# Attention for one query, forward and backward: another order of DRAM blocks over the SBUF partitions

## The chip, the core and the metric

The kernel runs on one NeuronCore of a Trainium2 chip. Its time is the device time of one execution in microseconds (us). Three runs of the kernel before took 642.05, 642.48 and 642.67 us, so the median is 642.48 us.

The engines are TensorE (PE, matmul; its weight loads are listed as PEld), VectorE (DVE), ScalarE (ACT), GpSimd (POOL) and SyncE (SP). In this kernel SP does nothing but issue DMAs. Sixteen DMA engines carry them out.

## The reference

For each of 32 heads there is one query row, 8192 key rows and 8192 value rows of 128 numbers in bf16. The output is the attention, and from the gradient of the output the gradients of q, k and v are computed:

```
scores = q . k^T * 128**-0.5        # 1 x 8192 for each head
p      = softmax(scores)
out_0  = p . v                      # 1 x 128
dp     = grad_out . v^T             # 1 x 8192
ds     = p * (dp - sum(p * dp)) * 128**-0.5
out_1  = dq = ds . k                # 1 x 128
out_2  = dk = ds^T x q              # 8192 x 128 for each head
out_3  = dv = p^T x grad_out        # 8192 x 128 for each head
```

K and V are read once and dK and dV are written once. Each of these four is 2 MB for a head and 67 MB in all. So 134 MB are read and 134 MB are written. The other arrays are 8 KB each.

All sums over keys run over all 8192 of them, and everything else is done for each key by itself. The order in which the keys lie on chip therefore does not matter, as long as K, V, dK and dV share it.

## The kernel before

One head's K is a tile `Kt` of 128 partitions with `NT` = 64 rows of 128 bf16 each, which is 16 KB in a partition. `Vt` (V), `G_dk` and `G_dv` (the gradients) have the same shape. `rows_of` (line 69) is the DRAM side of every transfer of these four: partition p holds the 64 rows from 64p on, a contiguous block of 16 KB, and the block of partition p + 1 follows it directly.

`load_k` and `load_v` (lines 77 and 83) issue the loads, one transfer of 2 MB for each head and tensor. Only the first K is loaded in four parts of 512 KB, each with 4 KB in a partition. `outer` (line 249) computes a gradient tile in four quarters on VectorE and stores it with one transfer of 2 MB; for the first and the last head it uses two of 1 MB, with 8 KB in a partition.

The loop over `h` runs through 33 steps. In step h the scores, the softmax, the products with V and dV of head h are computed; and for head h - 1 the rest: ds, dq and dK. The order of instructions on each engine is the order in which the code is written (`tc.manual_schedule`). SP's order of DMAs follows from it: in the steady part it is a load of K, a store of dK, a load of V, a store of dV.

There are three buffers for K and two each for V, `G_dk` and `G_dv`. A load waits until the last reader of its buffer is done (for K the matmuls of dq at line 231, for V the transposes at line 197 or the matmuls of the output). A store waits for VectorE's last quarter (line 256), and VectorE waits for a store to land before it writes that buffer again.

On chip the rows are worked on by `k_blocks` (line 162, 32x32 transposes on VectorE), `k_scores` (line 177), `v_transposes` (line 197), `v_scores` (line 207) and `contract` (line 231). They address partitions and slots of the tiles and never a place in DRAM.

Of the kernel before, what the change touches and what calls it, by code (L numbers as in the profile page):

```python
# [15 lines left out]
CH = 16  # L16
# [9 lines left out]
def kernel(  # L26
# [12 lines left out]
    P = 128  # L39
# [28 lines left out]

    def rows_of(x, h, c, parts):
        L = NT // parts  # L70
        return x[0, h].rearrange("(p n) d -> p n d", p=P)[:, c * L:(c + 1) * L, :]

    def slots(X, c, parts):
        L = NT // parts
# [2 lines left out]
    def load_k(h):  # L77
        Kt[h] = kpool.tile([P, NT, D], BF16, tag="K", name="Kt")
        parts = NCH if h == 0 else 1
        for c in range(parts):  # L80
            nc.sync.dma_start(slots(Kt[h], c, parts), rows_of(k, h, c, parts))

    def load_v(h):
        Vt[h] = vpool.tile([P, NT, D], BF16, tag="V", name="Vt")
        nc.sync.dma_start(Vt[h][:], rows_of(v, h, 0, 1))
# [163 lines left out]
    def outer(h, which, r):  # L249
        x = st[h]  # L250
        if r == 0:
            x[which] = gpool.tile([P, NT, D], BF16, tag=which, name="G_" + which)
        G, dst = x[which], out_2 if which == "dk" else out_3
        rep, row = x["ds"] if which == "dk" else x["p"], qd[h][:, 0 if which == "dk" else 1, :]
        Q = NT // 4
        nc.vector.tensor_tensor(  # L256
            slots(G, r, 4).rearrange("p n (a b) -> p n a b", b=R),
            slots(rep, r, 4).unsqueeze(2).to_broadcast([P, Q, D // R, R]),
            row.rearrange("p (a b) -> p a b", b=R).unsqueeze(1).to_broadcast([P, Q, D // R, R]),
            op=ALU.mult)  # L260
        parts = 1
        if h == 0 or h == H - 1:
            parts = 2
        if r % (4 // parts) == 4 // parts - 1:
            c = r // (4 // parts)
            nc.sync.dma_start(rows_of(dst, h, c, parts), slots(G, c, parts))
# [37 lines left out]
    for h in range(H + 1):  # L304
        p_ = h - 1
        if h < H:
            x = st[h] = {}
# [121 lines left out]
```

## Time and profile before

| | |
|---|---|
| median of three runs | 642.48 us |
| the profiled execution | 642.33 us |
| its span, first to last instruction | 640.5 us |
| VectorE busy | 546.7 us (85%) |
| TensorE busy | 466.5 us (73%) |
| ScalarE busy | 205.5 us (32%) |
| HBM read, written | 134.23 MB, 134.23 MB |
| packets of 16 KB in SP's queue | 15744 |

A profile has rows for the busy time of engines, for 40 equal slices of the span (each digit is the busy share in tenths), for the DMA queues with their packets and the share of the 16 DMA engines' time that these took, for the chain of work that ended last, and for groups of instructions by line. A transfer is split into packets, here one for each contiguous run, and the packets are shared out over the 16 DMA engines. The trace also holds one record for each packet with its start, its duration and its size, but not the engine that carried it.

### The profile page before, as it was taken

How to read it: one execution, taken by the hardware profiler on the slowest of the kernel's cores; microseconds unless marked ns; L12 is line 12 of the kernel's file. 1: busy time of each engine (PE TensorE's matmuls, PEld its weight loads, DVE VectorE, ACT ScalarE, POOL GpSimd, SP SyncE). 2: the span in 40 equal slices, each digit the busy share in tenths (PEclk: the TensorE clock that was granted, in tenths of full speed). 3: DMA queues.
4: the chain of work that ended last, by engine and by line, in shares of the span. 5: the costliest groups of instructions: out<-in, count | busy, mean ns of one | idle time of the engine just before them, and what ended most of it. 6: DMA issues, size and time to landing. Idle time of an engine off the chain costs nothing.

```text
span 640.5 us, 8426 instructions
## 1 busy us (share of the span) xinstructions
PE 466.5 (73%) x3336; PEld 276.5 (43%) x3336; DVE 546.7 (85%) x780; ACT 205.5 (32%) x507; POOL 7.1 (1%) x13
## 2 busy tenths in 40 slices
PE   3776778778877867887866867767877687676771
PEld 1444444445544533455533444434554344444351
DVE  6799999998999999988889888898888988889871
ACT  1433332234433322334421333313442133322240
POOL 4000000000000000000000000000000000000000
PEclk9979888887787899877899887898787888879875
DMA  8999999999999999999999999999999999999994
GB/s 353 421 415 427 429 431 426 425 433 426 429 431 427 429 431 427 430 429 429 431 427 432 428 425 437 427 424 436 428 425 435 428 426 434 426 430 433 427 405 193
DMA packets 19671, 269.01 MB, mean 420 GB/s; under 512 B 2352, under 2 KB 2352, under 8 KB 2864
## 3 DMA queue, kind: packets, MB, share of 16 engines
q1 hardware_dynamic: 19536, 268.46, 98.6%
q8 instruction: 26, 0.43, 0.3%
q14 instruction: 13, 0.11, 0.0%
q10 hardware_dynamic: 96, 0.02, 0.0%
HBM read 134.23 MB, written 134.23 MB: 419 GB/s over the span
## 4 chain that ended last, share of the span: by engine, by line
DMA 45%; DVE 39%; PE 9%; ACT 4%; issue 1%; DVEq 0%; ACTq 0%
DMA Kt<-in_k_dram 45%; DVE XK_sb L162 15%; DVE G_dv L256 9%; DVE G_dk L256 7%; PE s_ps L177 3%; DVE dpT L214 2%; PE T_ps L197 2%; PE acc_ds L231 2%; ACT XV_sb L188 2%; DVE sT L184 1%; ACT p_rep L371 1%; DVE prod L217 1%; DVE ds L285 1%; ACT qd L273 1%; DVE four L125 1%
## 5 line engine op out<-in xcount | busy, mean ns | idle before, releaser
L197 PE MATMUL T_ps<-ident_f,Vt 128*128 128x128 f32 x1024 | 178.0, 339 | 1.0 <-DMA Vt<-in_v_dram 0.4
L256 DVE TENSOR_TENSOR G_dv<-p_rep,qd 128x2048 bf16<-128x2048 bf16 x128 | 148.2, 1220 | 35.3 <-DMA out_dram<-G_dv 28.1
L177 PE MATMUL s_ps<-XK_sb,win_q 128*128 128x512 bf16 x512 | 135.8, 397 | 50.1 <-DVE XK_sb L162 26.3
L197 PEld LDWEIGHTS T_ps<-ident_f,Vt 128*128 128x128 f32 x1024 | 151.4, 177 | 28.5 <-issue 20.1
L256 DVE TENSOR_TENSOR G_dk<-ds_rep,qd 128x2048 bf16<-128x2048 bf16 x128 | 154.7, 1210 | 1.1
L188 ACT COPY XV_sb<-T_ps 128x512 f32<-128x512 f32 x256 | 138.4, 586 | 53.2 <-PE T_ps L197 52.6
L162 DVE STREAM_TRANSPOSE XK_sb<-Kt 128x1024 f32<-128x1024 f32 x128 | 151.4, 1221 | 3.1 <-DMA Kt<-in_k_dram 2.9
L177 PEld LDWEIGHTS <-win_q 128*128 128x128 bf16 x512 | 52.7, 105 | 123.8 <-issue 83.2
L290 ACT COPY win_ds<-ds 128x64 bf16<-128x64 bf16 x32 | 7.8, 244 | 193.0 <-DVE ds L285 193.0
L355 ACT ACTIVATE e<-sT,nbias 128x64 f32<-128x64 f32 x32 | 13.0, 406 | 138.4 <-DVE nbias L350 138.4
L343 PE MATMUL m_ps<-ident_f,top 128*128 128x128 f32 x32 | 11.0, 342 | 60.3 <-DVE top L341 57.3
L207 PE MATMUL dp_ps<-XV_sb,do_win 128*32 128x512 bf16 x512 | 34.0, 382 | 24.7 <-ACT XV_sb L188 24.7
L231 PE MATMUL acc_p<-Vt,win_p 128*32 128x512 bf16 x512 | 48.3, 516 | 0.5 <-ACT win_p L372 0.5
L343 PEld LDWEIGHTS m_ps<-ident_f,top 128*128 128x128 f32 x32 | 4.5, 139 | 74.4 <-DVE top L341 72.9
L231 PE MATMUL acc_ds<-Kt,win_ds 128*32 128x512 bf16 x512 | 33.5, 382 | 0.9 <-ACT win_ds L290 0.9
L207 PEld LDWEIGHTS <-do_win 128*32 128x32 bf16 x512 | 14.2, 94 | 36.0 <-issue 29.5
L369 DVE RECIPROCAL rinv<-m_ps 128x1 f32<-128x1 f32 x32 | 5.4, 168 | 24.9 <-ACT qd L273 24.9
L184 DVE STREAM_TRANSPOSE sT<-s_ps 128x512 f32<-128x512 f32 x32 | 22.7, 709 | 3.6 <-PE s_ps L177 3.6
L356 PE MATMUL m_ps<-rs,ones_f 128*128 128x1 f32 x64 | 15.4, 310 | 11.5 <-ACT e L355 11.5
L231 PEld LDWEIGHTS <-win_p 128*32 128x32 bf16 x512 | 13.1, 117 | 23.8 <-issue 12.2
L214 DVE STREAM_TRANSPOSE dpT<-dp_ps 128x512 f32<-128x512 f32 x32 | 21.6, 675 | 0.8 <-PE dp_ps L207 0.8
L356 PEld LDWEIGHTS m_ps<-rs,ones_f 128*128 128x128 f32 x64 | 14.0, 272 | 17.8 <-ACT e L355 17.3
(57 smaller groups left out, 203.3 us busy)
## 6 DMA issues: line engine op xcount, KB each, us to landing
Vt<-in_v_dram SPq DMA_DIRECT2D x32, 2048.0 KB, 29.5
Kt<-in_k_dram SPq DMA_DIRECT2D x31, 2048.0 KB, 31.6
out_dram<-G_dv SPq DMA_DIRECT2D x30, 2048.0 KB, 34.8
out_dram<-G_dk SPq DMA_DIRECT2D x30, 2048.0 KB, 32.2
out_dram<-G_dv SPq DMA_DIRECT2D x4, 1024.0 KB, 11.6
out_dram<-G_dk SPq DMA_DIRECT2D x4, 1024.0 KB, 11.7
Kt<-in_k_dram SPq DMA_DIRECT2D x4, 512.0 KB, 5.6
out_dram<-fin_sb SPq DMA_DIRECT2D x2, 8.0 KB, 12.1
```

Of the source, the lines that this page charges most:

```text
L162: nc.vector.transpose(XK[h][:, :, :, u, :], slots(Kt[h], u, NCH).rearrange("p g d -> p (g d)").bitcast(F32).rearrange("p (g w j) -> p g w ...
L177: nc.tensor.matmul(st[h]["s"][:], lhsT=q_win[h % 2][:, c, at:at + P], rhs=cols[:, c // 2, u, c % 2], start=(u == 0 and c == 0), stop=(u == ...
L184: nc.vector.transpose(sT[:].rearrange("p g r -> p (g r)"), x["s"][:])
L188: nc.scalar.copy(XV[h][:, c * TB:(c + 1) * TB, :], st[h].pop(("T", c))[:])
L197: nc.tensor.transpose(T_ps[:, i, :], words[:, m * P:(m + 1) * P], ident_f[:])
L207: nc.tensor.matmul(out[b * QD:(b + 1) * QD, :], lhsT=do_win[:, h, e2, 2 - 2 * z:2 - 2 * z + QD], rhs=cols[:, z, e2, :, b * QD:(b + 1) * QD ...
L214: nc.vector.transpose(x["dpT"][:].rearrange("p m r -> p (m r)"), x["dp"][:])
L231: nc.tensor.matmul(acc[which][b * QD:(b + 1) * QD, :], lhsT=window(h, which)[:, g, at:at + QD], rhs=X[:, 4 * g:4 * g + 4, :].rearrange("p ...
L256: nc.vector.tensor_tensor(slots(G, r, 4).rearrange("p n (a b) -> p n a b", b=R), slots(rep, r, 4).unsqueeze(2).to_broadcast([P, Q, D // R, ...
L343: nc.tensor.transpose(x["m"][:, 128:256], top[:].to_broadcast([P, P]), ident_f[:])
L355: nc.scalar.activation(e[:].rearrange("p (u g) -> p u g", u=NCH), x["sn"], ACT.Exp, bias=nbias[:], scale=scale, accum_out=rs[:])
L356: nc.tensor.matmul(x["m"][:, 0:1], lhsT=ones_f[:], rhs=rs[:], start=True, stop=True, skip_group_check=True)
```

## The change

One line of `rows_of` is changed. A head's 128 blocks of 16 KB are numbered 16b + a, with a from 0 to 15 and b from 0 to 7, and block 16b + a now lies in partition 8a + b. Before, block p lay in partition p. So partitions 8a to 8a + 7 hold eight blocks that lie 256 KB apart in DRAM, and the partitions b, 8 + b, 16 + b and so on hold sixteen neighbouring blocks. Loads and stores use the same function, so K, V, dK and dV are moved alike and the outputs stand where they stood in DRAM.

```diff
     def rows_of(x, h, c, parts):
         L = NT // parts
-        return x[0, h].rearrange("(p n) d -> p n d", p=P)[:, c * L:(c + 1) * L, :]
+        return x[0, h].rearrange("(b a n) d -> a b n d", a=CH, b=P // CH)[:, :, c * L:(c + 1) * L, :]
```

`CH` is 16 and `P` is 128. The DRAM side of a transfer was one count of 128 with a contiguous run in it; it is two nested counts, 16 and 8, with the same run. The SBUF side is still 128 partitions. The words of the change are: "Partition 8a+b holds rows of DRAM block 16b+a: each DMA engine's 16 KB blocks lie 256 KB apart, neighbouring engines 16 KB apart".

## The prediction

> **What bounds the kernel now.** I read the busy shares of the engines first, then the DMA share slice by slice, then the queue's row, then the chain that ended last, and last the single packets.
>
> The head of the page, and its DMA rows:
>
> ```profile
> span 640.5 us, 8426 instructions
> PE 466.5 (73%) x3336; PEld 276.5 (43%) x3336; DVE 546.7 (85%) x780; ACT 205.5 (32%) x507; POOL 7.1 (1%) x13
> ...
> DMA  8999999999999999999999999999999999999994
> GB/s 353 421 415 427 429 431 426 425 433 426 429 431 427 429 431 427 430 429 429 431 427 432 428 425 437 427 424 436 428 425 435 428 426 434 426 430 433 427 405 193
> DMA packets 19671, 269.01 MB, mean 420 GB/s; under 512 B 2352, under 2 KB 2352, under 8 KB 2864
> ...
> q1 hardware_dynamic: 19536, 268.46, 98.6%
> ```
>
> VectorE is the busiest compute engine with 85%, but the DMA row is at 9 from the second slice to the last but one, and SP's queue (q1) keeps the 16 DMA engines busy for 98.6% of the span. The rate stands at 424 to 437 GB/s from the fourth slice to the 38th. So the kernel is bound by the time its packets take on the 16 engines, and VectorE has 94 us of slack.
>
> The chain of waits says the same:
>
> ```profile
> DMA 45%; DVE 39%; PE 9%; ACT 4%; issue 1%; DVEq 0%; ACTq 0%
> ```
>
> The 39% of VectorE is shared credit: where the chain follows VectorE through a head, the queue behind it is full as well. The stretches show it, in order: PE, PEld, DVE, ACT, POOL busy, then the clock, the DMA share and GB/s:
>
> ```profile
> 20.00:100.00 80.00, 59.52 (x451) 35.10 (x451) 73.60 (x104) 29.30 (x72) 0.00 (x0) 0.89 1.01 424
> 100.00:300.00 200.00, 156.54 (x1131) 93.87 (x1131) 182.55 (x262) 67.55 (x167) 0.00 (x0) 0.85 1.01 429
> 300.00:500.00 200.00, 148.36 (x1077) 88.98 (x1076) 170.72 (x242) 65.60 (x161) 0.00 (x0) 0.87 1.01 429
> 500.00:620.00 120.00, 88.86 (x613) 51.43 (x613) 101.92 (x146) 36.93 (x89) 0.00 (x0) 0.84 1.00 428
> 620.00:640.00 20.00, 4.58 (x36) 3.34 (x35) 6.20 (x10) 2.11 (x8) 0.00 (x0) 0.60 0.57 237
> ```
>
> A DMA share of 1.00 to 1.01 over 600 us leaves no hole (packets overlap by some ns, hence the 1.01). Only the end has room: 0.57 in the last 20 us. How deep the queue is, by the issues (KB each, us to landing):
>
> ```profile
> Vt<-in_v_dram SPq DMA_DIRECT2D x32, 2048.0 KB, 29.5
> Kt<-in_k_dram SPq DMA_DIRECT2D x31, 2048.0 KB, 31.6
> out_dram<-G_dv SPq DMA_DIRECT2D x30, 2048.0 KB, 34.8
> out_dram<-G_dk SPq DMA_DIRECT2D x30, 2048.0 KB, 32.2
> ```
>
> A 2 MB transfer is 128 packets of 16 KB, 8 for each engine. The trace's packet records give 15744 of 16 KB, median 611 ns, mean 614 ns, 98% of them between 600 and 625 ns, loads and stores alike. Eight take 4.9 us, so 30 to 35 us to landing are six to seven transfers in the ring: the engines never wait for SP. 16 KB in 611 ns is 26.8 GB/s an engine, 429 for sixteen, which is the page's rate.
>
> **The change, part by part.** It alters one function, the DRAM view that the K and V loads and the dK and dV stores use. The same 135 transfers are issued by SP in the same order with the same bytes; PE, VectorE, ScalarE and GpSimd get the same instructions. Keys and values are permuted alike, so no compute is added. Three things can cost.
>
> (1) Issue. The DRAM side is now two nested counts (16 by 8) and a 16 KB run, where it was one count of 128. If SP's issue grew from 0.34 us (an issue's usual time in the timeline) to the largest seen, 1.1 us, 135 of them would take some 100 us more of SP's time over the whole run: under a ring of 30 us that is hidden. Bounds 0 and, for the first load alone, 0.8 us; I take 0. Without the deep ring it would be at most 100 us.
>
> (2) DRAM order. Runs stay 16 KB long, so the packets stay 15744. What a packet costs beyond 611 ns sums to 3.1 us an engine now; 52 of the 15744 took over 900 ns. From below: all of it goes, -3.1 us. From above: every packet is a slow one, about 1010 ns, a factor 1.65. Nearest is the common row: the rate is the same flat 611 ns for reads of DRAM and for writes to it, which does not look like a price set by DRAM. I take 0. [...]
>
> (3) Which partitions an engine serves. This is where I see the price. Before, both sides of a transfer count 128. Now the DRAM side's outer count is 16, and as the change's own words have it, engine a has block group a, which is partitions 8a to 8a+7, a run of eight in order. [...] From below: nothing, 611 ns stay. From above: two engines are sent through what one of them fills now, all the time, and each packet takes 2 x 611 = 1222 ns. No row of the trace shows two engines on one path, so the ends are far apart. I choose near the upper one: the flat 611 ns in both directions points to a limit on the engine's SBUF side, that is the side which is regrouped, and sixteen streams at 429 GB/s show that no two of them share it now.
>
> [...]
>
> The factor. If two engines walk four packets on one path and four on the next, one ahead of the other by d packets, they collide for 4 - d of each four: the time is (2 x (4 - d) + d) / 4 = 2 - d/4 of the old one. Where two share equally, a lead neither grows nor shrinks. In the trace the sixteen packet starts lie spread over one packet's time (at 300 us: 300.02 to 300.63), so two engines differ by a third of a packet on the mean, up to one. I take d = 0.4: factor 1.9; the ends are 1 and 2.
>
> **The sum,** made against the profiled execution: 642.33 us, of which the span is 640.5 and 1.8 lies around it; the median of the runs is 642.48, 0.02% above, so no correction. In the packet records the stream lasts 637.1 us from first packet to last end; an engine idles 8.6 us of it (7.5 of these in the last 25 us), leaving 628.5 us busy. Fixed: 8.6 idle + 1.8 before the first packet + 1.6 after the last + 1.8 around the span = 13.8. Check: 628.5 + 13.8 = 642.3. After: 628.5 x 1.9 + 13.8 = 1208 us. Compute is hidden: VectorE's 547 us fit more easily, and it will wait for loads that land after some 30 x 1.9 = 57 to 66 us instead of 30 to 35.
>
> **The rivals.**
> *No sharing: not slower.* The path that limits to 611 ns is the DMA engine's own, whichever partitions it serves. For it: the same figure for loads and stores, and in every stretch. Against it: sixteen such engines would need sixteen free paths after the change as before. Time: 642, or 639 if the 3.1 us of slow packets go (faster by 0.5%). It decides as soon as two engines that share can both keep 611 ns. 13 in 100; within it 3 for a gain, 8 for no change, 2 for a small loss.
> *Half the sharing.* Only one direction collides (loads write SBUF, stores read it, and these are half and half: 134.23 MB each), or the pairs drift apart by d = 2 packets and more through slow packets of 400 ns extra: factor 1.5, 628.5 x 1.5 + 13.8 = 957 us. For it: 52 irregular packets exist. Against it: a fast pair waits for the slowest one at each transfer's end, which puts it back in step. 17 in 100, over 1.3 to 1.7.
> *DRAM order.* Sixteen engines in one 256 KB window meet in the same places of DRAM, packets go to 1010 ns: 628.5 x 1.65 + 13.8 = 1051 us. For it: the slow packets that exist; against it: 429 GB/s do not depend on direction or stretch. 7 in 100.
> *The forecast,* factor 1.75 to 2: 1114 to 1271 us, 60 in 100. More than 2: 3 in 100.
>
> **How the numbers follow.** The likeliest is 1208. The range takes the forecast, the DRAM case and the upper part of half-sharing (from a factor of 1.43): 915 to 1280, leaving out 13 for no sharing, some 5 for factors under 1.43, and 3 above. Its own range is 1114 to 1271. About 0.2% (1.3 us) is what a measurement here can tell from no change; by the cases faster 0.03, same 0.08, slower 0.89.
>
> **What would show it.** Right: GB/s of about 225 in the middle slices with a DMA share still at 9 and 1.0; 16 KB packets with a common length near 1222 ns and, where leads exist, some at 611; landing near 60 us; VectorE's share near 45% with idle before L162 and L256 put down to DMA; SP's issues still near 0.34 us. No sharing: packets at 611 and 429 GB/s. Half: two kinds of packets, or landing times of loads and stores that part. DRAM: packet times that scatter widely instead of standing near a multiple of 611. What makes the forecast wrong: an engine's eight packets that are not partitions 8a to 8a+7, or an SBUF side with room for two engines.

## The result and the profile after

The changed kernel is slower by 8.6%: the ratio to the kernel before is 1.0856 (95% interval 1.0820 to 1.0892). The median of six executions is 700.59 us, against 642.58 us. The forecast was 1208 us with a range from 915 us, so the direction was right and the size was far off.

One thing is needed to read the numbers. The executions of the changed kernel differ among themselves, 692.24 to 722.78 us, where those of the kernel before lie between 642.05 and 642.73. The profiled execution is the longest of them, 722.78 us with a span of 721.0, and the interval leaves the two longest out. Why they differ is a part of the explanation below.

The head of the page and its DMA rows, of the changed kernel:

```profile
span 721.0 us, 8426 instructions
PE 487.6 (68%) x3336; PEld 281.8 (39%) x3336; DVE 547.5 (76%) x780; ACT 206.1 (29%) x507; POOL 7.4 (1%) x13
...
DMA  8999999999999999999999999999999999999975
GB/s 206 216 250 272 263 328 315 316 337 343 351 398 410 412 391 423 422 429 428 427 428 420 423 417 408 415 426 423 432 428 425 428 421 425 414 417 413 352 226 245
DMA packets 19671, 269.01 MB, mean 373 GB/s; under 512 B 2352, under 2 KB 2352, under 8 KB 2864
...
q1 hardware_dynamic: 19536, 268.46, 98.3%
```

The same packets and bytes, the same VectorE time (547.5 us, 546.7 before), and DMA engines that are as busy as before: 98.3% of a longer span. So the packets themselves have become longer. The GB/s row shows where. The first two slices run at 206 and 216 GB/s, which is half of the 429 of before. Then the rate climbs for some 250 us, stays between 408 and 432 for almost 400, and falls back to 226 at the end.

The chain that ended last is now mostly a wait for K:

```profile
DMA 76%; PE 11%; DVE 10%; ACT 1%; issue 0%; DVEq 0%
```

The same stretches in figures (us, the engines' busy times, the clock, the DMA share, GB/s):

```profile
0.00:36.00 36.00, 18.19 (x101) 10.27 (x102) 19.24 (x30) 9.45 (x23) 7.41 (x13) 0.86 0.95 211
36.00:108.00 72.00, 43.06 (x302) 25.25 (x301) 49.85 (x72) 18.49 (x45) 0.00 (x0) 0.82 1.01 278
108.00:250.00 142.00, 93.96 (x628) 54.92 (x627) 101.08 (x144) 38.63 (x94) 0.00 (x0) 0.78 1.01 360
250.00:650.00 400.00, 292.82 (x2038) 168.48 (x2040) 334.00 (x477) 123.49 (x305) 0.00 (x0) 0.84 1.01 421
650.00:721.00 71.00, 39.55 (x279) 22.92 (x271) 43.37 (x61) 15.99 (x40) 0.00 (x0) 0.74 0.82 307
```

Against 429 GB/s these five stretches lose 18, 25, 23, 8 and 20 us (for instance 72 x (1 - 278 / 429) = 25), 94 in all. The kernel before loses 13 us in the same way, 12 of them in its first and last 20 us (367 and 237 GB/s there). The difference of 81 us is the whole difference of the spans (80.5). Some seven tenths of the loss (66 of 94 us) lie in the first 250 us.

The packet records say what became longer. Of the 15744 packets of 16 KB, 12438 still take 600 to 625 ns; 1878 take over 900 ns, against 52 before; the mean is 689 ns, against 614. Of the packets that start 10 to 40 us after the first one, the median is about 1262 ns: twice 611.

What VectorE waits for, in the two kernels' groups (idle before, and what ended it), is a small part of this. Before:

```profile
L162 DVE STREAM_TRANSPOSE XK_sb<-Kt 128x1024 f32<-128x1024 f32 x128 | 151.4, 1221 | 3.1 <-DMA Kt<-in_k_dram 2.9
```

After:

```profile
L162 DVE STREAM_TRANSPOSE XK_sb<-Kt 128x1024 f32<-128x1024 f32 x128 | 151.8, 1223 | 44.9 <-DMA Kt<-in_k_dram 44.9
L256 DVE TENSOR_TENSOR G_dv<-p_rep,qd 128x2048 bf16<-128x2048 bf16 x128 | 148.2, 1221 | 40.7 <-DMA out_dram<-G_dv 32.4
```

The transposes of K wait 44.9 us for the load instead of 2.9.

SP's issues did grow, from 0.34 to 0.55-0.59 us, in the changed kernel's timeline (start, us, what):

```profile
399.66 0.59 SPq L81 DMA_DIRECT2D Kt<-in_k_dram  x1
404.08 0.55 SPq L266 DMA_DIRECT2D out_dram<-G_dk  x1
410.75 0.59 SPq L85 DMA_DIRECT2D Vt<-in_v_dram  x1
411.58 0.55 SPq L266 DMA_DIRECT2D out_dram<-G_dv  x1
```

The DMA share of 1.00 and more beside it shows that this is hidden.

### The profile page after: what moved, and what is told of

The parts are those of the page before. It is cut to its first block, busy times and chain, and to the rows that moved or that the text cites. A ratio compares the mean times of both kernels' runs of the same rounds, so it can differ in the third digit from the quotient of the medians.

```text
span 721.0 us, 8426 instructions
## 1 busy us (share of the span) xinstructions
PE 487.6 (68%) x3336; PEld 281.8 (39%) x3336; DVE 547.5 (76%) x780; ACT 206.1 (29%) x507; POOL 7.4 (1%) x13
## 3 DMA queue, kind: packets, MB, share of 16 engines
q1 hardware_dynamic: 19536, 268.46, 98.3%
## 4 chain that ended last, share of the span: by engine, by line
DMA 76%; PE 11%; DVE 10%; ACT 1%; issue 0%; DVEq 0%
DMA Kt<-in_k_dram 76%; DVE XK_sb L162 7%; PE s_ps L177 7%; PE acc_ds L231 2%; DVE G_dk L256 1%; DVE dpT L214 1%; DVE G_dv L256 1%; PE T_ps L197 0%; PE m_ps L245 0%; ACT XV_sb L188 0%; DVE prod L217 0%; PE acc_p L231 0%; PE m_ps L277 0%; DVE sT L184 0%; PE dp_ps L207 0%
## 5 line engine op out<-in xcount | busy, mean ns | idle before, releaser
L177 PE MATMUL s_ps<-XK_sb,win_q 128*128 128x512 bf16 x512 | 162.5, 460 | 86.4 <-DVE XK_sb L162 68.3
L197 PE MATMUL T_ps<-ident_f,Vt 128*128 128x128 f32 x1024 | 175.9, 336 | 26.3 <-DMA Vt<-in_v_dram 26.2
L162 DVE STREAM_TRANSPOSE XK_sb<-Kt 128x1024 f32<-128x1024 f32 x128 | 151.8, 1223 | 44.9 <-DMA Kt<-in_k_dram 44.9
L197 PEld LDWEIGHTS T_ps<-ident_f,Vt 128*128 128x128 f32 x1024 | 148.6, 174 | 53.3 <-issue 40.2
L177 PEld LDWEIGHTS <-win_q 128*128 128x128 bf16 x512 | 59.1, 118 | 176.7 <-issue 150.0
L343 PE MATMUL m_ps<-ident_f,top 128*128 128x128 f32 x32 | 10.4, 325 | 62.7 <-DVE top L341 62.3
L231 PE MATMUL acc_p<-Vt,win_p 128*32 128x512 bf16 x512 | 45.2, 488 | 0.9 <-ACT win_p L372 0.9
L231 PEld LDWEIGHTS <-win_ds 128*32 128x32 bf16 x512 | 10.8, 96 | 21.5 <-ACT win_ds L290 14.4
```

Of the source, the lines that this page charges most:

```text
L162: nc.vector.transpose(XK[h][:, :, :, u, :], slots(Kt[h], u, NCH).rearrange("p g d -> p (g d)").bitcast(F32).rearrange("p (g w j) -> p g w ...
L177: nc.tensor.matmul(st[h]["s"][:], lhsT=q_win[h % 2][:, c, at:at + P], rhs=cols[:, c // 2, u, c % 2], start=(u == 0 and c == 0), stop=(u == ...
L197: nc.tensor.transpose(T_ps[:, i, :], words[:, m * P:(m + 1) * P], ident_f[:])
L231: nc.tensor.matmul(acc[which][b * QD:(b + 1) * QD, :], lhsT=window(h, which)[:, g, at:at + QD], rhs=X[:, 4 * g:4 * g + 4, :].rearrange("p ...
L343: nc.tensor.transpose(x["m"][:, 128:256], top[:].to_broadcast([P, P]), ident_f[:])
```

## The experiments

**Is it the order in DRAM, or the way the engines are given partitions?** Two kernels part the two. The first takes the 16 by 8 counts of the change but leaves each group's blocks where the kernel before has them, only backwards within eight, since in forward order the two counts could be written as one count of 128:

```diff
-        return x[0, h].rearrange("(b a n) d -> a b n d", a=CH, b=P // CH)[:, :, c * L:(c + 1) * L, :]
+        return x[0, h].rearrange("(a b n) d -> a b n d", a=CH, b=P // CH)[:, ::-1, c * L:(c + 1) * L, :]
```

> The DRAM blocks stay with their engines' neighbourhood as before the change: partitions 8a to 8a+7 hold blocks 8a+7 down to 8a (one contiguous 128 KB window for each group of eight, groups 128 KB apart, as in the kernel before); but the DRAM side counts 16 by 8, as in the changed kernel. Theory 'shared path' (the outer count of 16 gives each engine eight partitions in a row, and two engines then meet on one SBUF path): as slow as the changed kernel, 690 to 725 us, with the first slices near 210 GB/s and many packets near 1222 ns. Rival 'DRAM order' (the 256 KB steps or the 16 KB between neighbours cost the time): 642 us, all packets at 611 ns.

Measured: 711.32 us, ratio 1.104 (1.099 to 1.110), and the rate starts like that of the changed kernel:

```profile
GB/s 210 215 279 260 315 339 386 413 425 427 428 402 422 420 425 429 428 428 426 429 425 425 409 351 345 354 353 323 357 349 327 312 321 317 316 293 312 246 176 219
```

So the loss is there without the scattered DRAM order. This profiled execution (768 us, the longest of four) also shows that the good state can be lost again: after the 22nd slice the rate falls from 425 to 350 and then 300.

The second keeps a scatter much like that of the change, with counts 32 by 4:

```diff
-        return x[0, h].rearrange("(b a n) d -> a b n d", a=CH, b=P // CH)[:, :, c * L:(c + 1) * L, :]
+        return x[0, h].rearrange("(b a n) d -> a b n d", a=2 * CH, b=P // (2 * CH))[:, :, c * L:(c + 1) * L, :]
```

> Almost the DRAM scatter of the change, with another outer count: partition 4a+b holds block 32b+a, so the DRAM side counts 32 by 4 instead of 16 by 8. Blocks of neighbouring groups are still 16 KB apart and those within a group are 512 KB apart. Theory 'shared path': with groups of four partitions the engines can keep separate paths, so 642 to 643 us and 429 GB/s from the first slices on. Rival 'DRAM order': slow like the changed kernel, 680 us or more.

Measured: 643.03 us, ratio 1.0011 (1.0002 to 1.0021).

```profile
GB/s 334 420 425 426 433 421 428 426 430 428 428 430 428 430 427 431 428 429 429 429 428 430 430 425 432 430 427 430 429 428 428 431 426 426 434 428 426 433 403 193
DMA packets 19671, 269.01 MB, mean 420 GB/s; under 512 B 2352, under 2 KB 2352, under 8 KB 2864
```

With blocks 512 KB apart inside a group and neighbours 16 KB apart, the scattered DRAM order costs about 0.1% (at most 0.2%). So the loss goes with the outer count of 16 and not with the order in DRAM; this pair settles that. What the count changes on the way is not seen: the packet records name neither an engine nor a partition.

**Loads, stores, or both?** The change on one direction alone, by a second view for the other:

```diff
+    def rows_plain(x, h, c, parts):
+        L = NT // parts
+        return x[0, h].rearrange("(p n) d -> p n d", p=P)[:, c * L:(c + 1) * L, :]
...
-            nc.sync.dma_start(rows_of(dst, h, c, parts), slots(G, c, parts))
+            nc.sync.dma_start(rows_plain(dst, h, c, parts), slots(G, c, parts))
```

The stores-alone kernel puts `rows_plain` into `load_k` and `load_v` instead. In both, loads and stores no longer agree on the order of the tokens, so rows of the results land in other places; packets and bytes stay.

> The change on the loads alone; the stores keep the order of before, so the rows of dK and dV land in permuted places and those two outputs are not the reference's. Theory 'shared path, both directions': a part of the loss, 655 to 690 us, with the first 20 us (which are only loads) at 210 GB/s. Rival 'only writes into SBUF meet': the whole loss, 690 to 725 us, and nothing with stores alone.

> The change on the stores alone; the loads keep the order of before, so dK and dV land in permuted places here too. Theory 'shared path, both directions': a part of the loss, 655 to 690 us, with the first 20 us at the rate of before (353 GB/s and more) and slow packets only once stores run. Rival 'only writes into SBUF meet': 642 to 644 us.

Measured: loads alone 711.93 us (ratio 1.097, 1.093 to 1.101), stores alone 661.68 us (1.032, 1.026 to 1.038). Neither expectation fits as a whole: loads alone cost as much as the whole change, as the rival had it, yet stores alone are not free. The GB/s rows of loads alone and of stores alone (the first is of the longest of four executions, 856 us, where the others took 703 to 717):

```profile
GB/s 209 219 263 275 321 307 351 317 374 410 413 426 428 417 352 322 331 331 298 305 338 321 316 314 327 315 309 302 306 303 298 301 305 294 314 301 298 252 205 203
```

```profile
GB/s 357 407 388 385 401 403 409 418 415 428 424 427 428 421 423 430 427 428 427 422 428 429 420 424 420 421 427 429 427 423 425 413 421 426 429 420 418 420 373 202
```

The first 20 us hold only loads. They run at half rate in the one kernel and at 357 to 407 in the other. But in both the rate moves over time, so these totals are no prices of a load or a store in step.

**The price in step.** To keep the engines in step, SP is made to wait until all rings are empty at the end of each head but the first, by two tiny loads into the same tile, of which the second waits for the first:

```diff
+    drain = consts.tile([16, D], BF16, name="drain")
...
+        if h > 0:
+            for i in range(2):
+                nc.sync.dma_start(drain[:], q[0, 0:16, 0, :])
         if h == H - 1:
```

First on the changed kernel, then on the kernel before and on the two halves of the change:

> The changed kernel with two tiny loads (4 KB in all, over all 16 engines) at the end of each head; the second has to wait for the first, so SP issues nothing more until every engine has emptied its ring, and all engines start the next head together. Theory 'engines a and a+4 meet, and only the drift apart saved the changed kernel': the whole run stays at the rate of its start, 210 to 260 GB/s, 1050 to 1270 us, near the factor 1.9 of the prediction. Rival 'the slow start fades by itself': 700 to 780 us, the changed kernel's time and some 32 bubbles of 2 us.

> The kernel before with the same draining at the end of each head, as the base for the three drained variants: what the 32 empty rings cost by themselves. Where engines never meet it is 642 us and some 1.5 to 4 us for each head: 690 to 770 us, all packets near 611 ns. If it came out near 1052 us, the draining and not the meeting made the drained changed kernel slow.

> The change on the loads alone, drained at the end of each head (dK and dV rows permuted as with loads alone). Theory A, drawn from the first 20 us of the loads-alone run (209 GB/s) and its plateau near 300: loads that meet take twice the time, stores hardly more, so in step most of the drained loss comes from here: 4.9 us more for each of 62 loads, 304 us above the drained kernel before at most, 930 to 1040 us. Theory B (loads and stores meet alike): about half of the drained loss, 860 to 900 us.

> The change on the stores alone, drained at the end of each head. Theory A (from the rate of 385 to 409 GB/s in the early slices of the stores-alone run, that is some 5.8 us for a store instead of 4.9): 20 to 80 us above the drained kernel before. Theory B (loads and stores meet alike): about half of the drained loss, 860 to 900 us.

| drained kernel | us | above drained before | mean 16 KB packet, ns |
|---|---|---|---|
| before | 789.87 | | 659 |
| stores changed | 903.77 | 113.9 | 748 |
| loads changed | 1035.90 | 246.0 | 913 |
| both changed | 1052.48 | 262.6 | 925 |

The changed kernel, drained, and the GB/s row of the kernel before, drained:

```profile
DMA  9998899888999889998888988989888899888976
GB/s 209 228 282 239 279 279 245 270 246 261 275 276 254 272 233 269 272 267 263 260 239 268 283 237 249 238 272 286 243 263 218 267 289 239 269 225 263 288 190 211
...
GB/s 369 418 383 349 314 299 325 405 315 309 329 345 407 311 315 309 348 389 297 311 332 373 352 337 331 346 335 389 313 326 324 350 363 324 300 314 399 318 322 320
```

In the drained changed kernel the rate never climbs: 218 to 289 GB/s from the third slice to the 38th, where the kernel that is not drained reached 429. So the changed kernel's recovery is not a matter of warming up; it is lost as soon as the engines are put in step again. Draining by itself costs 147 us (789.87 against 642.51), more than the 50 to 130 expected, so the base is not clean: its rings stand empty for a part of the time (DMA share 0.86 between 200 and 600 us), and its packets are longer too (659 ns in the mean, 614 without draining). Divided by 64 transfers of 2 MB each way, the differences would be 3.8 us more for a load (246.0 / 64) and 1.8 us for a store (113.9 / 64), on 4.9 us. The expectation for the stores, 20 to 80 us in all, was too low. But the two do not add up (360 against 263), so they are no prices yet.

**Loads and stores, packet by packet.** The packet records settle what these totals leave open. On a busy engine the next packet mostly starts within 4 ns of the end of the one before, and each transfer gives every engine eight packets and then one of 4 bytes (2192 of these in the kernel before, 16 for each of SP's 137 transfers). So the packets can be strung into sixteen chains, one for each engine, and the order in which SP issues tells a load from a store. The mean 16 KB packet, over the heads in which the chains are complete (23 to 28 of them):

| drained kernel | load, ns | store, ns |
|---|---|---|
| before | 715 | 611 |
| stores changed | 774 | 725 |
| loads changed | 1176 | 636 |
| both changed | 1176 | 638 |

In step, a changed load takes 1.9 times 611 ns, and a changed store beside it hardly more than before. Against the drained kernel before this is 8 x (1176 - 715) = 3.7 us for a load and 0.2 us for a store, or 242 of the 263 us over 62 loads and 62 stores. With the stores alone changed the stores do become longer, and so do the plain loads; why, no run shows. In the changed kernel without draining it is the loads as well: between 18 and 690 us the packets of an engine take 70 us more than 611 ns each would, and 63 of these are in loads.

**Who meets whom, and what a lead does.** The packet records do not name the engine. Loads with outer counts of 12 and 4 are meant to give some engines more to do than others before the first K. Which engines take them, and which pairs meet, as the expectations put it, are assumptions of the author's; the chains of the lead-of-four kernel show only groups of four, eight and four. The lead of four:

```diff
+    lead = gpool.tile([P, NT, D], BF16, tag="dv", name="lead")
+    nc.sync.dma_start(lead[0:48], v[0, 0].rearrange("(b a n) d -> a b n d", n=NT, a=32)[0:12, 0:4])
+    nc.sync.dma_start(lead[64:80], v[0, 0].rearrange("(b a n) d -> a b n d", n=NT, a=32)[0:4, 0:4])
     load_k(0)
```

The others have `0:2` for a lead of two, `[0:8, 0:4]` alone for the lead of one half over the other, and `0:8` for a lead of eight, there with `a=16` and tiles of 96 and 32 partitions. The last run is the lead of four once more, with `parts = 1` in `load_k`: the first K comes in one transfer of 2 MB and not in four of 512 KB.

> The changed kernel with two small loads of V blocks into an unused buffer ahead of everything: 4 packets of 16 KB for each of the first 12 engines, then 4 more for the first 4. Engines 0-3 start 8 packets late, 4-7 and 8-11 start 4 late, 12-15 at once. Theory 'engines a and a+4 meet, four packets at a time': every such pair is 4 packets apart, so nobody meets: 400 GB/s and more from about the second slice on (the changed kernel had 216), and 645 to 670 us although eight packets (4.9 us) are added. Rival 'the slow start is something else in the new access pattern, and fades by itself': first slices at 206 to 270 GB/s as before, 692 to 728 us.

> As with the lead of four, but 2 packets each, so that each pair a, a+4 is 2 packets apart. Theory 'engines a and a+4 meet': the prediction's formula gives the factor 2 - 2/4 = 1.5, that is 429 / 1.5 = 286 GB/s in the slices after the first, and a time between the changed kernel's and that of the lead of four: 655 to 695 us. Rival 'fades by itself': 206 to 270 GB/s, 692 to 728 us.

> As with the lead of four, but 4 packets for each of engines 0-7 and none for 8-15: a and a+8 are apart, a and a+4 in step. Theory 'engines a and a+4 meet': no help, 206 to 270 GB/s in the first slices and 692 to 728 us. Rival 'a and a+8 meet, or any disorder between engines helps': 400 GB/s early, 645 to 670 us.

> As with the lead of four, but 8 packets each, a whole transfer between a and a+4. While the queue holds only loads (the first five transfers) such pairs meet again, so the first two slices should stay near 210 to 260 GB/s. Once loads and stores alternate, one of a pair loads while the other stores. If a load and a store do not meet: 400 GB/s and more from the fourth slice on, 660 to 685 us with 9.8 us of added packets. If they do meet: the slow climb of the changed kernel, 700 to 735 us.

> [...] Theory 'engines a and a+4 meet, four packets at a time': now the first transfers run apart too, 350 GB/s or more in the second and third slice, where the lead of four had 256 and 255; in all 645 to 685 us. Rival 'a lead of four is too narrow to hold while loads and stores follow each other, whatever the first load does': 250 to 300 GB/s there and 675 to 700 us.

GB/s by stretch, and the median and range of the times:

| | 20-40 us | 40-60 | 60-80 | 80-100 | 100-140 | us |
|---|---|---|---|---|---|---|
| changed | 214 | 268 | 274 | 278 | 327 | 700.59 (692 to 723) |
| a against a+8, four | 218 | 267 | 241 | 307 | 317 | 709.58 (701 to 727) |
| a against a+4, two | 265 | 309 | 332 | 385 | 421 | 696.53 (685 to 703) |
| a against a+4, four | 252 | 306 | 334 | 397 | 402 | 693.37 (678 to 701) |
| the same, first K in one load | 289 | 325 | 378 | 377 | 416 | 681.38 (674 to 694) |
| a against a+4, eight | 243 | 247 | 397 | 429 | 429 | 684.11 (683 to 686) |

Every lead that was meant to part a from a+4 goes with higher rates between 60 and 140 us and, but for the lead of eight from 40 to 60 us, also before. Each row is one execution, though, and the times for leads of two and four overlap with those of the changed kernel. A lead of four did not give the free start that the formula promises, not even with the first K in one load (285 and 320 GB/s in the second and third slice, 350 expected); and a lead of two did as well as four. The chains show that these leads were in place: between 25 and 45 us the engines of the lead-of-four kernel stand in groups of four, eight and four, the first two groups 4 to 5 packets apart and the last two 1 to 2, and yet their packets take 1034 ns in the mean. With the lead of two it is 1002 ns, in the changed kernel 1234. So the formula 2 - d/4 does not hold while all engines load.

The lead of one half over the other, however, was no test. Its sixteen engines begin the first V within 0.8 us of each other (13.96 to 14.75 us), which is less than one of their packets there, so the lead was gone before the first long packet. By the same assumptions the other leads put a and a+8 as far apart as a and a+4. So it is not shown that the partner is four engines away and not eight, nor what disorder of another kind would do.

The lead of eight gave the clearest answer. Its GB/s row and its issues in the first 80 us:

```profile
GB/s 184 246 221 342 403 430 427 429 427 430 427 427 424 429 428 427 429 429 423 425 429 428 426 425 429 428 426 424 425 428 410 417 425 425 418 421 413 411 304 198
```

```profile
22.06 0.54 SPq L81 DMA_DIRECT2D Kt<-in_k_dram  x1
45.93 2.83 SPq L269 DMA_DIRECT2D out_dram<-G_dv  x2
48.86 0.59 SPq L85 DMA_DIRECT2D Vt<-in_v_dram  x1
58.54 0.55 SPq L269 DMA_DIRECT2D out_dram<-G_dk  x1
59.15 0.59 SPq L81 DMA_DIRECT2D Kt<-in_k_dram  x1
```

As long as only loads are queued it is slow like the others. From the time when stores stand between the loads (from 46 us on, L269 is the store line here) the rate climbs, is 430 within three slices and stays above 400 until the 38th slice. In the chains at 100 us, eight engines load and the eight others, about a transfer away, store; all sixteen are in the first four of their eight packets, and no packet takes more than 614 ns. So a load and a store hardly hinder each other here. Nor is there one limit for all loads together: later in this run 12 to 14 engines at times load at once, at 613 to 639 ns a packet. It is also the only one of these kernels that is steady: four times between 683 and 686 us. Its rest of 42 us above the kernel before lies mostly in the first four slices, the added packets and the last two slices, where the queue runs dry (304 and 198 GB/s). The stretch of loads alone is longer in it: the first stores are issued at 45.93 us, in the changed kernel at 28.59.

## Why the prediction was wrong

**What held.** That the price goes with the regrouped counts and not with DRAM order or issue: shown by the outer count of 32, which costs 0.1%, and by the backward blocks, which cost 10.4% without scatter. DRAM was put at 0, and the +0.1% of the 32 by 4 kernel bears it out. SP's issue went to 0.55-0.59 us, not the 0.34 given as a sign, but within the bounds of part 1, and it is hidden. Engines that load in step take twice as long in the changed kernel: 206 and 216 GB/s at the start, 1262 ns a packet, against the 1222 of the upper bound. In the sum, compute was hidden as said, and the packets' longer time (709 us for each engine after, 631 before) makes 77 of the 80 us between the two profiled executions.

The reason given, two engines on one path into SBUF, fits this but was not seen. The lead of eight agrees with it in so far as eight engines that load and eight that store, about a transfer away, keep to 614 ns a packet and less at 100 us; the lead of four does not, with 1034 ns a packet; and no run shows which engine meets which.

**What failed** is the factor 1.9, in two steps of its working.

The first is the sentence that where two share equally, "a lead neither grows nor shrinks", and with it d = 0.4 for the whole run. The reading behind d cannot carry it: engines that are never idle have their sixteen starts within one packet's time, however many whole packets lie between them. Counted along the chains, the foremost and the hindmost engine of the kernel before are 1.1 packets apart at 25 us, 8.6 at 300 us and 17.8 at 600 us. So engines drift apart even without the change. In the changed kernel they are 1.1 packets apart at 25 us, 5.2 at 100 us and 26.5 at 300 us, and the rate climbs meanwhile. The factor on the stream that follows from the profiled execution is (722.78 - 13.8) / 628.5 = 1.13, and 1.09 from the median; yet it was 2 at the start.

The step before it also took the wrong reach: the collisions were thought to come back every eight packets, but since a load hardly hinders a store, as the lead of eight shows (at most 614 ns a packet at 100 us), a pair that is about a transfer apart is out of reach in the steady alternation. This would explain why the good state holds for hundreds of us once reached, and why the times scatter: how soon the engines get there, and whether they fall back as in the backward-blocks profile, differs from execution to execution. No run shows it pair by pair. With the drift prevented by draining, the time is 1052 us, inside the range that was given; but draining alone costs the kernel before 147 us, so this agreement is partly luck.

The second is that both directions were priced alike, 0.9 x 4.9 = 4.4 us for each transfer. In step a load's packet takes 1176 ns, near the 1.9 x 611 of the forecast, but a store's takes 638, nearly the price of before. The two together are a factor of about 1.5; so even without drift 1.9 was too much.

No run shows the walk from path to path that the factor's formula assumes. What the runs showed between 25 and 45 us is 1234 ns a packet without a lead, 1002 ns with a lead of two and 1034 ns with a lead of four, where 2 - d/4 times 611 gives 1222, 917 and 611.

The rival called half the sharing (957 us) named both steps as alternatives: that only one direction collides, as the drained kernels show of the loads, and that pairs drift apart. Its time was too long as well, since the drift went on until hardly any price was left. The argument set against it, that a fast pair waits for the slowest at each transfer's end, did not hold: with six to seven transfers in the ring the engines run three to four transfers apart (26.5 packets at 300 us, 35.4 at 500). It can hold only where the ring empties, as in the drained changed kernel, which stays at 218 to 289 GB/s.

**What stays open:** whether the longer packets come from a path that two engines share or from something else that goes with the count of 16, and which engines meet; how much of the drift comes from irregular packets, as the kernel before has them too, and how much from an uneven share of the path; why a lead of two or four helps, but less than the formula says; and why stores alone, drained, take 725 ns. That the engine numbers are what the lead loads assume was not seen in a record; the chains only show groups of four, eight and four.

## What to carry to other kernels

The outer count on the DRAM side of a transfer mattered here though packets and bytes stayed the same: with 128 partitions, outer counts of 128 and of 32 kept 429 GB/s, and an outer count of 16 halved it at the start (206 GB/s). Why was not shown: the packet records name neither an engine nor a partition. When a queue is saturated, look at the length of the packets and at the first slices, not at the DMA share, which was 98% in the fast and in the slow kernel alike. And when a contention is priced, ask whether the parties stay in step for the whole run: here, with six to seven transfers in the ring, the engines drifted 26.5 packets apart by 300 us, and this gave back most of a factor of two.

## What the runs showed that was not expected

- A saturated queue can heal itself: 206 GB/s in the first slice and 429 by the 18th, with no change in the work.
- Loads and stores at the same time hardly disturb each other (423 to 430 GB/s from the sixth slice to the 30th at a lead of eight), while changed loads in step take 1262 ns a packet instead of 611, and stores beside them, in the drained kernel, 638.
- The engines of a saturated queue do not stay in step even in the kernel before: 1.1 packets from the first to the last at 25 us, 17.8 at 600 us.
- Emptying the rings once a head, 31 times, cost the kernel before 147 us, 4.8 us each time.
